# Fewer changes of TensorE tile shape per visit, and two constants moved, in an attention-then-MLP kernel

## The chip, the cores and the metric

The kernel runs on one core of a Trainium2 chip. The metric is the device time of one execution in microseconds (us). A profile of one more execution gives the span from the first to the last instruction, the busy time of each engine and every instruction's start. The engines are named PE (TensorE; PEld is its weight load), DVE (VectorE), ACT (ScalarE), POOL (GpSimd) and SP (SyncE, which here only issues transfers).

## What is computed

The reference is an attention of two parts for 64 heads (8 batches of 8 heads, 576 positions, 64 columns), summed, followed by an MLP with a SiLU gate on 4608 tokens of 512 columns.

```python
q_d, k_d, v_d = means of 4 neighbouring rows of q, k, v        # 144 positions
out_up    = repeat(softmax(q_d k_d^T / 8) v_d, 4)              # every 4 rows alike
mask      = abs(i - j) < 4                                     # a band, 576 x 576
out_local = softmax(where(mask, q k^T / 8, -1e9)) v
x   = (out_up + out_local) as (4608, 512)
h   = x @ w_in            # 512 -> 2048
out = (h * sigmoid(h)) @ w_out    # 2048 -> 512
```

## The kernel before

Heads go in pairs: 32 pairs p, each with its two heads h on the two halves of the 128 partitions. A pair passes through these steps. T(p) transposes q and k on TensorE into two banks of PSUM, which are evicted to qT and kT, and DVE or POOL sums groups of four columns into qd and kd. S(p) makes the band's scores and the coarse scores in the two banks of AB, and ACT takes the exponentials (Pt, Pd). Z(p) sums the exponentials with matmuls by 0/1 columns, and DVE takes the reciprocals of the sums (zr, 72 columns). PV(p) multiplies by v into the two banks of CD, and DVE multiplies CD by the reciprocals Rb, spread to all the rows that need them. POOL adds the two parts into xT, the MLP's input. VP(p) makes the coarse v of the first 14 pairs.

The whole plan is written as units with what they read and write; a list scheduler with estimated costs puts the units of each engine in an order before the program is made. A unit of an engine waits for what was written or read before it in the order in which the units were made. That holds for banks of PSUM too: the next writer of AB waits for the last reader of AB.

A matmul's tile shape (rows x columns of the array that it takes) follows from its operands. Half of the partitions on both sides gives 64x64, of which four run side by side. A whole contraction into half of the output gives 128x64. The MLP's matmuls are 128x128. S and PV before:

```python
def pe_S(u, p):
    ...
    for i in range(5):                       # the band: 20 matmuls of 64x64
        for h in range(2):
            for y in range(2):
                ...
                mm(u, AB[half(y), h, c:c + n], kT[j][half(h), t:t + 64], qT[j][half(h), t:t + n], rl, [rAB[h]])
    for h in range(2):                       # coarse, 4 of 64x64, 72 columns
        for y in range(2):
            mm(u, AB[half(y), h, 432:504], kd[j][half(h), 128:192], qd[j][half(h), 72 * y:72 * y + 72], rd, [rAB[h]])
    for h in range(2):                       # coarse, 2 of 64x128, 144 columns
        mm(u, AB[:, h, 288:432], kd[j][half(h), 0:128], qd[j][half(h), :], rd, [rAB[h]])

def pe_main(u, pv, z):
    ...
    if z is not None:                        # Z: 14 matmuls of 128x64 into CD[:, 0, 360:432]
        ...
    if pv is not None:                       # PV
        for y in range(2):                   # 4 of 128x64
            for h in range(2):
                mm(u, CD[half(h), y, 288:360], vd[n][:, 2 * h, :], Pd[m][:, h, 72 * y:72 * y + 72], rd, [rCD[y]], ...)
        for h in range(2):                   # 4 of 64x64
            for j in range(2):
                mm(u, CD[half(h), j, 288:360], vd[n][half(j), 2 * h + 1, :], Pd[m][half(j), h, 144:216], rd, [rCD[j]], ...)
        for i in range(5):                   # 20 of 64x64
            ...
```

How the reciprocals get spread depends on the pair. Pairs below NDIR = 8 split zr into three bf16 parts (one cast on ACT, three operations on DVE), and RB(p) spreads the parts by ten matmuls of 128x128 into AB, from where ACT copies them to Rb. For the others ACT's queue sends zr to memory and reads it back twice, once for each half of the partitions; the second transfer waits for the first, on ACT's own instruction stream.

```python
if p < NDIR:
    one("DVE", f"r{p}", ..., e.reciprocal(zs, CD[:, 0, 360:432]), ...)
    one("ACT", f"rh{p}", ...)       # h = bf16(zs)
    one("DVE", f"rx{p}", ...)       # the rest
    one("DVE", f"rm{p}", ...)       # m = bf16(rest)
    one("DVE", f"rl{p}", ...)       # l
    return
one("DVE", f"r{p}", ..., e.reciprocal(zr[i][:, :], CD[:, 0, 360:432]), ...)
dma("ACT", f"z{p}", scr[u][0:74, :], zr[i][0:74, :], ...)
for h in range(2):
    dma("ACT", f"b{p}", Rb[u][half(h), :], src, ..., r=[R(f"scr{u}")])
...
def RB(p):
    for m in range(10):
        mm(u, AB[:, x, 72 * c:72 * c + 72], sel[:, m, :], rpart[p % 2][:, 2, :], ..., [rAB[x]])
    one("ACT", f"eb{p}", 0.77, ... Rb[n] <- AB ..., r=rAB, w=[R(f"Rb{n}0"), R(f"Rb{n}1")])
```

The eviction of qT goes by ACT for pairs below NEQ = 8 and by DVE for the others: `eng = "ACT" if p < NEQ else "DVE"`. It reads the bank o0, which the second MLP matmul (G2) accumulates in as well.

Ten first rounds make the steps as single units (S(n), T(n+1), Z(n-1), PV(n-2), RB(n-1), VP(n-1) and, from n = 5, some of the first MLP matmuls G1). From n = 10 on, a visit n holds one unit V(n) and then MLP work:

```python
while todo or todo2:
    if n < NPAIR + 2:
        V(n)                 # S(n), T(n+1), Z(n-1), PV(n-2) in one unit
        if n <= NVP:
            VP(n - 1)
        feed()
    G1(1); G2((0,)); G1(1); G2((1,)); G1(1); G2((2, 3)); G1(1)
    n += 1
```

Of the kernel before, what the change touches and what calls it, by code (L numbers as in the profile page):

```python
# [16 lines left out]
NSUP = 9  # L17
XR = 1536
NVP = 14
NDIR = 8  # L20
NEQ = 8
NMQ = 8


# [251 lines left out]
def bass_hourglass_attn__then__act_silu_kernel(  # L276
# [9 lines left out]
    with kctx:  # L286
# [175 lines left out]
        def dma(eng, name, out_, in_, w, sem, dcost, r=(), prio=None, cost=0.42):  # L462
            return one(eng, name, cost, lambda s: s.dma_start(out_, in_), r, w, sem, prio, dcost)  # L463

        def load_qk(p):
            i = p % NQK
            ek = "ACT" if p < 1 else "SP"
            if p == 0:
                dma("ACT", "lkx", Rb[NR - 1][64:128, 0:576], bass.AP(tensor=k.tensor, offset=k.offset,
                                                                   ap=[[576, 64], [1, 576]]),  # L470
                    [R(f"Rb{NR - 1}1")], "kx", 0.5, prio=-20)
            dma("SP", f"lq{p}", qk[i][:, 0, :], bass.AP(tensor=q.tensor, offset=q.offset + 128 * p * 576,
                                                        ap=[[576, 128], [1, 576]]),
                [R(f"qk{i}0")], f"qk{i}0", 0.85, prio=10 * p)
            n = 128 if p < NPAIR - 1 else 64
            dma(ek, f"lk{p}", qk[i][0:n, 1, :], bass.AP(tensor=k.tensor, offset=k.offset + (128 * p + 64) * 576,
                                                          ap=[[576, n], [1, 576]]),
                [R(f"qk{i}1")], f"qk{i}1", 0.85, prio=10 * p)

        def load_v(p):  # L480
            i = p % NVS
            for h in range(2):
                n = 2 * p + h
                base = v[n // H_, n % H_]
                for j in range(2):
                    lo, hi = 0, 5
                    off = (288 * j - 3) * D_
                    w = [R(f"vs{i}{h}{j}")]
                    d = vs[i][half(j), 5 * h:5 * h + 5, :]
                    if n == 0 and j == 0:  # L490
                        lo = 1
                        one("DVE", "zero", 0.15, lambda g, d=d: g.memset(d[:, 0, :], 0.0), w=w)
                        first = bass.AP(tensor=base.tensor, offset=base.offset, ap=[[64, 61], [1, 64]])
                        dma("SP", f"lv{p}e", vs[i][3:64, 0, :], first, w, f"vs{i}{h}{j}", 0.3, prio=10 * p + 15)
                    if n == 2 * NPAIR - 1 and j == 1:
                        hi = 4
                        last = bass.AP(tensor=base.tensor, offset=base.offset + 517 * D_, ap=[[64, 59], [1, 64]])
                        dma("SP", f"lv{p}e", vs[i][64:123, 9, :], last, w, f"vs{i}{h}{j}", 0.3, prio=10 * p + 15)
                    win = bass.AP(tensor=base.tensor, offset=base.offset + off + 58 * 64 * lo,
                                  ap=[[64, 64], [58 * 64, hi - lo], [1, 64]])  # L500
                    dma("SP", f"lv{p}", d[:, lo:hi, :], win, w, f"vs{i}{h}{j}", 0.46, prio=10 * p + 15)

        def load_vq(p):
            b, h = divmod(2 * p, H_)
            i = p % NVQ
            base = v[b, h]
            t, o = base.tensor, base.offset
            dma("SP", f"lvq{p}", vq[i][:, 0:4:2, :],
                bass.AP(tensor=t, offset=o, ap=[[256, 128], [S_ * D_, 2], [1, 256]]),
                [R(f"vqm{i}")], f"vq{i}", 1.0, prio=10 * p + 21)  # L510
            for j in range(2):
                dma("SP", f"lvq{p}", vq[i][64 * j:64 * j + 16, 1:4:2, :],
                    bass.AP(tensor=t, offset=o + 128 * 256, ap=[[256, 16], [S_ * D_, 2], [1, 256]]),
                    [R(f"vqe{i}{j}")], f"vqe{i}{j}", 0.12, r=[R(f"vqc{i}1"), R(f"vqc{i}3")], prio=10 * p + 21)

        def load_w(c):
            if c < 4:
# [80 lines left out]
        def pe_S(u, p):  # L598
            j = p % NT
            rl = [R(f"kT{j}"), R(f"qT{j}"), R(f"kTp{j}0"), R(f"kTp{j}579")]  # L600
            rd = [R(f"kd{j}"), R(f"qd{j}"), R(f"kdp{j}")]
            for i in range(5):
                for h in range(2):
                    for y in range(2):
                        c, n = 58 * i, 58 if i < 4 else 56
                        t = 288 * y + c
                        mm(u, AB[half(y), h, c:c + n], kT[j][half(h), t:t + 64],
                           qT[j][half(h), t:t + n], rl, [rAB[h]])
            for h in range(2):
                for y in range(2):  # L610
                    mm(u, AB[half(y), h, 432:504], kd[j][half(h), 128:192], qd[j][half(h), 72 * y:72 * y + 72],
                       rd, [rAB[h]])
            for h in range(2):
                mm(u, AB[:, h, 288:432], kd[j][half(h), 0:128], qd[j][half(h), :], rd, [rAB[h]])

        def after_S(p):
            m = p % NP_
            one("ACT", f"x{p}", 0.66, lambda e: e.activation(Pt[m][:, :, :], AB[:, :, 0:288], AF.Exp, scale=0.125),  # L618
                r=rAB, w=[R(f"P{m}")])
            one("ACT", f"xd{p}", 0.54, lambda e: e.activation(  # L620
                Pd[m][:, :, :], AB[:, :, 288:504], AF.Exp, scale=0.0078125), r=rAB, w=[R(f"Pd{m}")])
            one("DVE", f"k{p}", 0.46, lambda e: e.tensor_tensor(
                Pt[m][:, :, :], Pt[m][:, :, :], mask_bf[:, :].unsqueeze(1).to_broadcast([128, 2, 288]), ALU.mult),
                r=[R(f"P{m}"), R("mask0"), R("mask1")], w=[R(f"P{m}")])
# [22 lines left out]
        def pe_main(u, pv, z):  # L647
            fresh = set()

            def first(x, h):  # L650
                f = (x, h) not in fresh
                fresh.add((x, h))
                return f

            if z is not None:
                m = z % NP_
                CD, rCD = acc(z)
                for s in range(4):
                    for h in range(2):
                        mm(u, CD[half(h), 0, 360:432], ohl[:, 63 - s:127 - s] if s else ohf[:, :],  # L660
                           Pt[m][:, h, 72 * s:72 * s + 72],
                           [R("ohl0"), R("ohl1"), R("ohf0"), R("ohf1"), R(f"P{m}")], [rCD[0]],
                           start=first(0, h), stop=False)
                for y in range(2):
                    for h in range(2):
                        mm(u, CD[half(h), 0, 360:432], ohp[:, 59 - 5 * y:123 - 5 * y], Pd[m][:, h, 72 * y:72 * y + 72],
                           [R("ohp"), R(f"Pd{m}")], [rCD[0]], start=False, stop=False)
                for h in range(2):
                    mm(u, CD[half(h), 0, 360:432], ohe[:, :], Pd[m][:, h, 144:216],
                       [R("ohe0"), R("ohe1"), R(f"Pd{m}")], [rCD[0]], start=False, stop=True)  # L670
            if pv is not None:
                m, n = pv % NP_, pv % NV
                CD, rCD = acc(pv)
                rd = [R(f"vd{n}0"), R(f"vd{n}1"), R(f"Pd{m}")]
                for y in range(2):
                    for h in range(2):
                        mm(u, CD[half(h), y, 288:360], vd[n][:, 2 * h, :], Pd[m][:, h, 72 * y:72 * y + 72],
                           rd, [rCD[y]], start=first(y, h), stop=False)
                for h in range(2):
                    for j in range(2):  # L680
                        mm(u, CD[half(h), j, 288:360], vd[n][half(j), 2 * h + 1, :], Pd[m][half(j), h, 144:216],
                           rd, [rCD[j]], start=False, stop=True)
                for i in range(5):
                    for h in range(2):
                        for j in range(2):
                            a, e = 58 * i, min(58 * i + 58, 288)
                            mm(u, CD[half(h), j, a:e], vb[n][half(j), 5 * h + i, :],
                               Pt[m][half(j), h, a:e], [R(f"vb{n}"), R(f"P{m}")], [rCD[j]],
                               start=False, stop=True)

        def after_Z(p):
            i, u = p % 2, p % NR
# [154 lines left out]
        def feed():  # L847

            for p in range(NPAIR):
                for name, fn, need in (  # L850
# [6 lines left out]
                        made.add((name, p))  # L857
                    if (name, p) in made or (src and (src, p) not in made):
                        continue
                    if p >= need[1] and (need[0], p - need[1]) not in made:  # L860
                        continue
                    if name in ("lv", "lvq") and ("lqk", p) not in made:
# [45 lines left out]
        while todo or todo2:  # L908
            if n < NPAIR + 2:
                V(n)  # L910
                if n <= NVP:
                    VP(n - 1)
                feed()
# [47 lines left out]
```

## Time and profile before

| | us |
|---|---|
| median of 3 runs | 368.88 (368.44 to 374.78) |
| span of the profiled execution | 369.2 |
| PE busy | 340.1 |
| DVE busy | 224.1 |
| ACT busy | 178.0 |
| POOL busy | 156.7 |

Times in the profile are from the first instruction. Busy time is a mean over stages that differ: the first rounds (up to about 76 us), the visits with attention and MLP (to about 290 us), and MLP alone. In a list of instructions in order of time each row has the start, the time to the end of the row's last instruction, the engine, the source line, the tiles (out<-in), the tile shape and operand, the number of instructions, and in brackets the idle time of the engine before it and what ended it. Matmuls are pipelined, so rows overlap; the distance between starts is what a step costs.

### The profile page before, as it was taken

To read this page: it belongs to the slowest core of one execution; us is meant where nothing else is said; L and a number is where in the kernel's file an instruction comes from. 1 tells how busy PE (TensorE), PEld (TensorE's weight loads), DVE (VectorE), ACT (ScalarE), POOL (GpSimd) and SP (SyncE) were. 2 spreads that over 40 slices of the span, in tenths; PEclk is the share of its full clock that TensorE was granted. 3 is DMA by queue.
4 is the path that set the end of the run, shared out by engine and by line. 5 is a ranking of instruction groups with operands and counts; after the bars stand their busy time and mean duration, and the time that the engine had idled before them with its cause. 6 is when DMAs were issued, how large, how long until landed. Compare 5 with 4: busy or idle time off the path is not lost.

```text
span 369.2 us, 10834 instructions
## 1 busy us (share of the span) xinstructions
PE 340.1 (92%) x4658; PEld 219.0 (59%) x4658; DVE 224.1 (61%) x390; ACT 178.0 (48%) x318; POOL 156.7 (42%) x203
## 2 busy tenths in 40 slices
PE   1684799889799999999999999999999999999996
PEld 0463577556466666666656666666656656666542
DVE  7574889877456677776777767777755343433400
ACT  3773677544255555445554554544443444443421
POOL 7838965543435555645565667453112100000000
PEclk9999589999899999999999999999999999999999
DMA  8898999999998767787768785322212110010012
GB/s 237 223 276 243 306 281 248 242 237 254 242 241 224 217 185 227 205 227 208 208 189 230 179 216 152 110 73 72 72 72 84 56 57 30 28 57 30 28 57 85
DMA packets 73977, 61.05 MB, mean 165 GB/s; under 512 B 48202, under 2 KB 56010, under 8 KB 73930
## 3 DMA queue, kind: packets, MB, share of 16 engines
q1 hardware_dynamic: 63818, 44.27, 44.9%
q10 hardware_dynamic: 5888, 9.80, 9.6%
q0 software_dynamic: 4224, 6.29, 7.5%
q8 instruction: 36, 0.59, 0.7%
q14 instruction: 11, 0.09, 0.1%
HBM read 52.49 MB, written 9.95 MB: 169 GB/s over the span
## 4 chain that ended last, share of the span: by engine, by line
PE 78%; DMA 8%; DVE 8%; POOL 2%; ACT 2%; ACTq 1%; issue 1%; POOLq 0%; DVEq 0%
PE HP L358 34%; PE o L358 25%; PE pe_ L358 8%; DMA scr<-zr 5%; PE CD L358 5%; PE AB L358 4%; DMA qk<-in_k_dram 3%; PE o L568 2%; POOL xo L381 2%; DVE rrest L702 1%; DVE gT L776 1%; DVE xo L736 1%; ACTq L463 1%; DVE rp L705 1%; DVE kd L582 1%
## 5 line engine op out<-in xcount | busy, mean ns | idle before, releaser
L358 PE MATMUL HP<-xT,w_in_sb 128*128 128x512 f32 x576 | 163.6, 421 | 1.1 <-DVE rp L705 1.0
L776 DVE SCALAR_TENSOR_TENSOR gT<-th,HP 128x512 bf16<-128x512 f32 x144 | 96.2, 683 | 102.3 <-ACT th L774 102.0
L774 ACT ACTIVATE th<-HP 128x512 f32<-128x512 f32 x144 | 85.9, 599 | 80.7 <-PE HP L358 78.8
L358 PEld LDWEIGHTS HP<-xT,w_in_sb 128*128 128x128 f32 x576 | 107.1, 192 | 27.6 <-DVE rp L705 1.1
L358 PE MATMUL o<-w_out_bf,gT 128*128 128x512 bf16 x464 | 107.2, 380 | 0.0
L358 PEld LDWEIGHTS o<-w_out_bf,gT 128*128 128x128 bf16 x464 | 42.4, 98 | 55.0 <-issue 9.5
L760 POOL TENSOR_TENSOR xT<-xo 128x576 fp32r<-128x576 f32 (+3 forms) x48 | 44.4, 938 | 51.3 <-DVE xo L736 51.1
L550 POOL CAST vb<-vs 128x640 bf16<-128x640 f32 x30 | 21.6, 719 | 68.1 <-PE CD L358 56.1
L791 ACT ACTIVATE osb<-o 128x512 f32<-128x512 f32 x29 | 17.3, 598 | 66.5 <-PE o L358 57.1
L540 POOL CAST qkb<-qk 128x1152 bf16<-128x1152 f32 x30 | 34.4, 1146 | 7.6 <-DMA qk<-in_k_dram 6.8
L568 PE MATMUL o<-idn,qkb 64*64 64x64 bf16 x576 | 17.4, 205 | 17.0 <-POOL qkb L540 7.5
L736 DVE TENSOR_TENSOR xo<-CD,Rb 128x720 f32<-128x720 f32 x30 | 27.1, 902 | 3.7 <-DMA Rb<-scr 2.3
L358 PE MATMUL pe_<-w_out_bf,gT 128*128 128x512 bf16 x112 | 26.4, 380 | 0.0
L568 PEld LDWEIGHTS o<-idn,qkb 64*64 64x64 bf16 x576 | 13.3, 117 | 20.6 <-POOL qkb L540 8.3
L578 ACT ACTIVATE kT<-pe_ 128x576 bf16<-128x576 bf16 x32 | 20.9, 654 | 8.6 <-PE pe_ L568 5.1
L555 POOL TENSOR_TENSOR vt<-vq 128x512 f32<-128x512 f32 x18 | 22.9, 1272 | 4.7 <-DMA vq<-in_v_dram 4.7
L582 DVE TENSOR_REDUCE kd<-kT 128x144 bf16<-128x576 bf16 x32 | 23.4, 734 | 1.5 <-ACT kT L578 1.5
L618 ACT ACTIVATE Pt<-AB 128x576 bf16<-128x576 f32 x32 | 20.8, 650 | 2.1 <-PE AB L358 1.9
L708 DVE RECIPROCAL zr<-CD 128x72 f32<-128x72 f32 x24 | 14.6, 607 | 8.4 <-PE CD L358 8.4
L568 PE MATMUL pe_<-idn,qkb 64*64 64x64 bf16 x576 | 16.7, 205 | 1.6 <-DVE qkb L537 1.0
L358 PEld LDWEIGHTS pe_<-w_out_bf,gT 128*128 128x128 bf16 x112 | 10.0, 98 | 13.6 <-issue 3.2
L586 DVE TENSOR_REDUCE qd<-qT 128x144 bf16<-128x576 bf16 x24 | 17.8, 743 | 0.0
(79 smaller groups left out, 313.8 us busy)
## 6 DMA issues: line engine op xcount, KB each, us to landing
vs<-in_v_dram SPq DMA_DIRECT2D x126, 80.0 KB, 4.2
qk<-in_q_dram SPq DMA_DIRECT2D x32, 288.0 KB, 4.6
out_dram<-osb SPq DMA_DIRECT2D x36, 256.0 KB, 2.9
qk<-in_k_dram SPq DMA_DIRECT2D x30, 288.0 KB, 5.2
Rb<-scr ACTq DMA_DIRECT2D x48, 180.0 KB, 4.4
vq<-in_v_dram SPq DMA_DIRECT2D x18, 256.0 KB, 5.3
w_in_sb<-in_moe_w_in_dram POOLq DMA_DIRECT2D x4, 1024.0 KB, 10.6
w_out_bf<-in_moe_w_out_dram POOLq DMA_DIRECT2D x4, 512.0 KB, 10.0
```

Source lines behind the costliest of these rows:

```text
L358: L.op(u, lambda t: t.matmul(out_, lhsT, rhs, start=start, stop=stop, skip_group_check=True), r, w)
L540: one("POOL", f"c{p}", 1.15, lambda g: g.tensor_copy(qkb[j][:, :, :], qk[i][:, :, :]), r=[R(f"qk{i}0"), R(f"qk{i}1")], w=[R(f"qkb{j}0"), R ...
L550: one("POOL", f"cw{p}", 0.72, lambda g: g.tensor_copy(vb[m][:, :, :], vs[i][:, :, :]), r=rr, w=[R(f"vb{m}")])
L555: one("POOL", f"va{p}", 1.3, lambda g: g.tensor_tensor(vt[:, :, :], vq[i][:, :, 0:128], vq[i][:, :, 128:256], ALU.add), r=rr, w=[R("vt")])
L568: L.op(u, lambda e, o=o, w=w, j=j: e.transpose(o, w, idn[half(j), :]), [R("id"), R(f"qkb{n}{x}")], [rE if x else rF])
L578: one("ACT", f"ek{p}", 0.68, lambda e: e.activation(kT[j][:, 3:579].rearrange("p (g r) -> p g r", r=9), pe_[:, 0:288].bitcast(BF16).rearra ...
L582: one("DVE", f"mk{p}", 0.74, lambda e: e.tensor_reduce(kd[j][:, 0:SD], kT[j][:, 3:579].rearrange("p (g r) -> p g r", r=4), AX.X, ALU.add), ...
L618: one("ACT", f"x{p}", 0.66, lambda e: e.activation(Pt[m][:, :, :], AB[:, :, 0:288], AF.Exp, scale=0.125), r=rAB, w=[R(f"P{m}")])
L736: one("DVE", f"m{p}", 0.92, prio=-450000 if L.boost else None, r=rCD + [R(f"Rb{u}0"), R(f"Rb{u}1")], w=[R(f"xo{x}")], fn=lambda e: e.tenso ...
L760: one("POOL", f"a{p}", 0.15 + n * 0.0019, lambda g, dst=dst, in0=in0, in1=in1: g.tensor_tensor(dst, in0, in1, ALU.add), r=[R(f"xo{x}")], w ...
L774: one("ACT", f"t{j}_{f}", 0.62, lambda e: e.activation(th[tb][:, :], hps[hb], AF.Tanh, scale=0.5), r=[rH[hb]], w=[R(f"th{tb}")], prio=-1)
L776: one("DVE", f"s{j}_{f}", 0.71, lambda e: e.scalar_tensor_tensor(gT[j % 2][:, f, :], th[tb][:, :], 1.0, hps[hb], ALU.add, ALU.mult), r=[rH ...
```

## The change

The change has three parts. It orders the matmuls of a visit by tile shape: in S the two matmuls of 64x128 become four of 64x64, and in the visit PV's 24 matmuls of 64x64 come ahead of Z, while PV's four of 128x64 come behind Z, whose shape they share. It raises NDIR from 8 to 10, so that pairs 8 and 9 are spread by TensorE as well (RB(9) is made right behind V(10)). It raises NEQ from 8 to 12, so that ACT evicts the q of pairs 8 to 11. A fourth piece would make the loads of late pairs wait (`tick`), from pair NTH on; with NTH = 99 and 32 pairs it never applies.

```diff
-NDIR = 8
-NEQ = 8
+NDIR = 10
+NEQ = 12
+NTH = 99
...
+        def tick(p, d):
+            return [R(f"tick{p - d}")] if p >= NTH else []
...                                     (tick(p, ...) added to the loads' reads)
             for h in range(2):
                 for y in range(2):
+                    mm(u, AB[half(y), h, 288:432], kd[j][half(h), 64 * y:64 * y + 64], qd[j][half(h), :], rd, [rAB[h]])
+            for h in range(2):
+                for y in range(2):
                     mm(u, AB[half(y), h, 432:504], kd[j][half(h), 128:192], qd[j][half(h), 72 * y:72 * y + 72],
                        rd, [rAB[h]])
-            for h in range(2):
-                mm(u, AB[:, h, 288:432], kd[j][half(h), 0:128], qd[j][half(h), :], rd, [rAB[h]])
...
+            if pv is not None:
+                ...
+                for h in range(2):
+                    for j in range(2):
+                        mm(u, CD[half(h), j, 288:360], vd[n][half(j), 2 * h + 1, :], Pd[m][half(j), h, 144:216],
+                           rd, [rCD[j]], start=first(j, h), stop=False)
+                for i in range(5):
+                    ...                         (the 20 band matmuls of PV, as before)
             if z is not None:
                 ...                             (Z, as before)
             if pv is not None:
                 ...
                 for y in range(2):
                     for h in range(2):
                         mm(u, CD[half(h), y, 288:360], vd[n][:, 2 * h, :], Pd[m][:, h, 72 * y:72 * y + 72],
-                           rd, [rCD[y]], start=first(y, h), stop=False)
-                ...                             (the 4 and the 20 matmuls of 64x64, moved up)
+                           [R(f"vd{n}0"), R(f"vd{n}1"), R(f"Pd{m}")], [rCD[y]], start=False, stop=True)
...
                 V(n)
+                if n <= NDIR:
+                    RB(n - 1)
                 if n <= NVP:
                     VP(n - 1)
```

More of the change, by code (lines that the diff above doesn't have):

```diff
@@ L473, in load_qk @@
                                                         ap=[[576, 128], [1, 576]]),
-                [R(f"qk{i}0")], f"qk{i}0", 0.85, prio=10 * p)
+                [R(f"qk{i}0")], f"qk{i}0", 0.85, r=tick(p, 4), prio=10 * p)
             n = 128 if p < NPAIR - 1 else 64
@@ L477, in load_qk @@
                                                           ap=[[576, n], [1, 576]]),
-                [R(f"qk{i}1")], f"qk{i}1", 0.85, prio=10 * p)
+                [R(f"qk{i}1")], f"qk{i}1", 0.85, r=tick(p, 4), prio=10 * p)
         def load_v(p):
@@ L500, in load_v @@
                                   ap=[[64, 64], [58 * 64, hi - lo], [1, 64]])
-                    dma("SP", f"lv{p}", d[:, lo:hi, :], win, w, f"vs{i}{h}{j}", 0.46, prio=10 * p + 15)
+                    dma("SP", f"lv{p}", d[:, lo:hi, :], win, w, f"vs{i}{h}{j}", 0.46, r=tick(p, 3), prio=10 * p + 15)
         def load_vq(p):
@@ L509, in load_vq @@
                 bass.AP(tensor=t, offset=o, ap=[[256, 128], [S_ * D_, 2], [1, 256]]),
-                [R(f"vqm{i}")], f"vq{i}", 1.0, prio=10 * p + 21)
+                [R(f"vqm{i}")], f"vq{i}", 1.0, r=tick(p, 3), prio=10 * p + 21)
             for j in range(2):
@@ L513, in load_vq @@
                     bass.AP(tensor=t, offset=o + 128 * 256, ap=[[256, 16], [S_ * D_, 2], [1, 256]]),
-                    [R(f"vqe{i}{j}")], f"vqe{i}{j}", 0.12, r=[R(f"vqc{i}1"), R(f"vqc{i}3")], prio=10 * p + 21)
+                    [R(f"vqe{i}{j}")], f"vqe{i}{j}", 0.12, r=[R(f"vqc{i}1"), R(f"vqc{i}3")] + tick(p, 3), prio=10 * p + 21)
         def load_w(c):
@@ L610, in pe_S @@
                 for y in range(2):
+                    mm(u, AB[half(y), h, 288:432], kd[j][half(h), 64 * y:64 * y + 64], qd[j][half(h), :], rd, [rAB[h]])
+            for h in range(2):
+                for y in range(2):
                     mm(u, AB[half(y), h, 432:504], kd[j][half(h), 128:192], qd[j][half(h), 72 * y:72 * y + 72],
                        rd, [rAB[h]])
-            for h in range(2):
-                mm(u, AB[:, h, 288:432], kd[j][half(h), 0:128], qd[j][half(h), :], rd, [rAB[h]])
         def after_S(p):
             m = p % NP_
+            made.add(("x", p))
             one("ACT", f"x{p}", 0.66, lambda e: e.activation(Pt[m][:, :, :], AB[:, :, 0:288], AF.Exp, scale=0.125),
-                r=rAB, w=[R(f"P{m}")])
+                r=rAB, w=[R(f"P{m}"), R(f"tick{p}")])
             one("ACT", f"xd{p}", 0.54, lambda e: e.activation(
@@ L653, in first @@
                 return f
+            if pv is not None:
+                m, n = pv % NP_, pv % NV
+                CD, rCD = acc(pv)
+                rd = [R(f"vd{n}0"), R(f"vd{n}1"), R(f"Pd{m}")]
+                for h in range(2):
[3 more added lines that the diff above has]
+                for i in range(5):
+                    for h in range(2):
+                        for j in range(2):
+                            a, e = 58 * i, min(58 * i + 58, 288)
+                            mm(u, CD[half(h), j, a:e], vb[n][half(j), 5 * h + i, :],
+                               Pt[m][half(j), h, a:e], [R(f"vb{n}"), R(f"P{m}")], [rCD[j]],
+                               start=False, stop=True)
             if z is not None:
@@ L673, in pe_main @@
                 CD, rCD = acc(pv)
-                rd = [R(f"vd{n}0"), R(f"vd{n}1"), R(f"Pd{m}")]
                 for y in range(2):
@@ L677, in pe_main @@
                         mm(u, CD[half(h), y, 288:360], vd[n][:, 2 * h, :], Pd[m][:, h, 72 * y:72 * y + 72],
-                           rd, [rCD[y]], start=first(y, h), stop=False)
[L679 to L689, printed above, removed]
+                           [R(f"vd{n}0"), R(f"vd{n}1"), R(f"Pd{m}")], [rCD[y]], start=False, stop=True)
         def after_Z(p):
@@ L859, in feed @@
                         continue
+                    if p >= NTH and name[0] == "l" and ("x", p - (4 if name == "lqk" else 3)) not in made:
+                        continue
                     if p >= need[1] and (need[0], p - need[1]) not in made:
```

## The prediction

> **What bounds the kernel now.** I read the slices of the page first, to see where TensorE is full.
>
> ```profile
> PE   1684799889799999999999999999999999999996
> DVE  7574889877456677776777767777755343433400
> PEclk9999589999899999999999999999999999999999
> ```
>
> Each digit is 9.2 us. From slice 11 (101 us) on PE has a 9 everywhere: the kernel ends when TensorE is through, and a nanosecond taken off PE there comes off the time. Before slice 8 it isn't full, and DVE shows 8 and 7. The granted clock falls twice, in slices 4 to 5 and in slice 10.
>
> Then the chain that ended last, for the stretch ahead of the full part and the first visits in it (start, length, what):
>
> ```profile
> 71.69 5.25 DMA scr<-zr
> 78.18 6.06 DMA scr<-zr
> 88.49 7.87 DMA scr<-zr
> 98.65 0.72 PE CD L358 x42
> 109.72 0.72 PE CD L358 x42
> 119.08 0.72 PE CD L358 x42
> ```
>
> Three transfers of reciprocals to memory stand in it, those of pairs 8, 9 and 10. From 98.65 on it is PE alone; the "CD x42" (Z and PV of one visit) come every 9 us or so, but the first distance is 11.07 us and the next 9.36.
>
> The instructions in order of time show what the third transfer does:
>
> ```profile
> 96.38 1.10 ACTq L463 DMA_DIRECT2D Rb<-scr  x2
> 97.52 0.60 ACT L791 ACTIVATE osb<-o 128x512 f32<-128x512 f32 x1 [6.69 <-issue]
> 98.17 0.21 PE L568 MATMUL o<-idn,qkb 64*64 64x64 bf16 x1 [2.48 <-ACT osb L791]
> ```
>
> ACT stands at the read-back, which waits for the landing, and is idle for 6.69 us. Behind it in ACT's order is the eviction that frees bank o0, in which visit 12's transposes want to write. PE idles 2.48 us. It is the only PE idle over 0.15 us after 76.29 us that I find until the end.
>
> Last, one visit on PE, with narrow windows so that the shapes come apart:
>
> ```profile
> 181.31 0.35 PE L358 MATMUL AB<-qT,kT 64*64 64x58 bf16 x20
> 181.49 0.21 PE L358 MATMUL AB<-qd,kd 64*64 64x72 bf16 x4
> ...
> 181.63 0.23 PE L358 MATMUL AB<-qd,kd 64*128 64x144 bf16 x2
> 181.79 0.21 PE L568 MATMUL o<-idn,qkb 64*64 64x64 bf16 x1
> ...
> 182.35 0.23 PE L358 MATMUL CD<-Pd,ohp 128*64 128x72 bf16 x4
> 182.41 0.20 PE L358 MATMUL CD<-Pd,ohe 128*64 128x72 bf16 x2
> 182.45 0.39 PE L358 MATMUL CD<-Pd,vd 128*64 128x72 bf16 x8
> ...
> 182.61 0.23 PE L358 MATMUL CD<-Pd,vd 64*64 64x72 bf16 x4
> 182.66 0.33 PE L358 MATMUL CD<-Pt,vb 64*64 64x58 bf16 x20
> 182.92 0.50 PE L358 MATMUL HP<-xT,w_in_sb 128*128 128x512 f32 x1
> ```
>
> Within one shape a step of 72 columns takes 0.03 us: four ohp, two at a time, from 182.35 to 182.41. Every change of shape has about 0.1 us more. From 181.49 to 181.63 there is one such step and 0.11 besides; 144 columns take twice 0.03, and from 181.63 to 181.79 there is 0.10 besides; two steps of vd should end at 182.51, and the 64x64 ones start at 182.61, 0.10 later. In addition the first four of the new shape hold up the next four: 182.61 to 182.66 is 0.05 instead of 0.03.
>
> [...] Here 2.48 us of idle were enough for the half clock of slice 10, and it costs the difference of the two distances above, 11.07 - 9.36 = 1.71 us. [...] the trace has 650 ns for the evictions of 576 columns on ACT, against 702 ns on DVE.
>
> **Part 1, the shapes.** A full visit before changes shape six times: 128x128 to 64x64 (S), 64x128, 64x64 (T), 128x64 (Z), 64x64 (PV), 128x128. After, three times: 64x64 (S, T, PV), 128x64 (Z, PV), 128x128. Gone are the three read above: 0.11 + 0.10 + 0.10 and twice 0.02 for the first four behind, less 0.01 for rounding: 0.34 us. The four 64x64 matmuls that take the place of two 64x128 run side by side in four quarters, so they take the same 0.06 us; I count nothing for them. Visits 11 to 30 are full: 20 x 0.34 = 6.8 us. Visit 31 has no T and goes from five changes to three: 0.24. Visits 32 and 33 have three either way. Visit 10 is in the full stretch of PE from its Z on (76.29 us): one change, 0.12. Sum 7.2 us, all on the path, as nothing in these visits lets PE idle.
>
> **Part 2, NDIR.** Pairs 8 and 9 no longer go through memory, but pair 10 still does. Its transfer took 7.87 us. Pair 9's read-backs, on the same queue, were issued at 84.26 and 84.75 and took 6.4 and 7.2 us, up to 92, so it stood behind them; pair 8's, with none in front of it, took 5.25. With some 5.25 the read-back would be issued near 93.8 and the eviction end near 95.5, just when PE arrives (95.7). I expect 85% of 2.48 + 1.71 = 4.2 us to go: 3.6 us.
>
> It costs: RB(9) is ten matmuls; the one of pair 7 took from 67.47 to 67.80, 0.33 us, at the same shape as its neighbours. I add 0.7 us in which PE waits for the third part of the reciprocals: the pairs before have such idle times of 0.21, 0.43, 0.53 and 0.96 us. Together 1.0.
>
> RB(8) is worse placed. It writes AB between S(9) and S(10), so visit 10 must wait for it and for ACT's copy out of AB (0.77 us). For pair 7 the reciprocal started at 61.45 and the third part was done at 66.25, 4.8 us. Pair 8's reciprocal starts at 71.05, so its third part comes at 75.85, RB at 76.2 and the copy with its hops at 77.2. S(10), which started at 73.86 before, starts at 77.3, and Z(9), which started at 76.29, comes 0.66 us behind it at 78.0: 1.7 us later. (From S to Z it is 182.20 - 181.31 = 0.89 us in the visit above, less the 0.23 us of S.) The MLP can't fill this: its first block is through by 74 us, its next one needs pair 7's x, and G2 needs a bank that visit 10's transposes use first.
>
> **Part 3, NEQ, and the first rounds.** From 58 to 77 us DVE is busy 16.6 of 19 us, ACT 10.7. Two evictions of 0.70 us leave DVE ahead of 71 us (in the rounds that make T(9) and T(10)), and one earlier (T(8)). Against it pair 8 brings DVE a mean of 0.86 + 0.27 + 0.65 = 1.8 us, but those are in the 4.8 us above already. S gets 0.24 us shorter in each round, where it is on the path only at times. I put 1.2 us for both: about half of the three evictions (1.0) and one S (0.2).
>
> Sum: -7.2 - 3.6 + 1.0 + 1.7 - 1.2 = -9.3. From 368.9 that makes **359.6 us**.
>
> **The rivals.** (a) The stop at visit 12 stays or moves to pair 10's new place, because the transfers are slow there for the other loads' sake (the DMA engines' share is 1.08 from 77 to 96 us). For it: 5.25 us is just the limit. Against it: pair 11's transfer, issued at 100.48, was followed by its read-back 3.9 us later. Then 3.6 us are lost: 363. (b) The wait for RB(8) brings a half clock of its own, 1.7 us or more, as 2.5 us of idle did twice: 361.5. Against it: RB and VP fall into that gap. (c) The handover at RB(8) is quicker, since ACT no longer stands still at 74.6 and DVE has two evictions less; then Parts 1 and 2 come whole: 356. (d) The shorter visits meet another bound, such as the reciprocals' way through memory, 11.5 us from zr at 174.08 to Rb at 185.6. Against it: CD must be free only 17 us after, and no engine but PE is over 72% busy from 103 to 223 us. Then perhaps 2 us of Part 1 are hidden: 361.6.
>
> **Range and chances.** Part 1 is read to some 0.02 us a visit, so it is good to 0.5 us. The rest has a spread of about 2.5 us, from (a) to (c). The range is 355.8 to 363.2. Two per cent are 7.4 us, a time of 361.5; Part 1 alone nearly gives that, and the rest is more likely a gain than a loss: 0.77 for faster, 0.22 for within 2%, 0.01 for slower.
>
> **What would show it.** In the profile after: full visits near 8.6 us apart in place of 8.96; no 64x128 group, and the 64x64 step ahead of the transposes without a 0.1 us hole; PE idle ahead of visit 10 with RB(8) or its copy as what ended it; no 2.48 us idle at visit 12 and no dip of the clock there; pair 10's transfer near 5 us. If the visits shrink by less than 0.3 us, Part 1 is wrong; if they do and the time is above 363, the stage from 70 to 100 us has a new stop.

## The result, and the profile after

| | us |
|---|---|
| before, median of 4 | 368.78 (368.44 to 374.78) |
| after, median of 4 | 360.38 (359.01 to 365.39) |
| ratio after to before | 0.976, 95% interval 0.973 to 0.979 |

The change makes the kernel 2.4% faster (2.1 to 2.7%). The medians are of all executions, while the ratios leave out those over 1.5% above the fastest of their kernel. The ratio times 368.8 is a gain of 8.7 us, between 7.7 and 9.9. The first profiled execution of the changed kernel was the longest of its timed ones (365.39 us), so the profile shown here is that of another execution of the same kernel (359.84 us, span 358.1).

The slices of the page, each 9.0 us wide now:

```profile
PE   1674899879999999999999999999999999999996
PEclk9995589999999999999999999999999999999999
```

The first digit is slice 0. PE is full from slice 9 on (81 us), before it was from slice 11, and the second dip of the clock is gone. The first is still there, in slices 3 and 4.

The chain that ended last (start, length, what), the Z and PV of visits 11 to 14:

```profile
86.15 0.61 PE CD L359 x39
95.19 0.61 PE CD L359 x39
104.30 0.61 PE CD L359 x40
113.34 0.61 PE CD L359 x40
```

The distances are 9.04, 9.11 and 9.04 us. Before, the distance from visit 12 to 13 was 11.07 and the next 9.36. No transfer of reciprocals stands in this stretch of the chain any more.

The instructions of one visit on PE, in order of time (visit 17; the transposes of T, from 139.20 on, are left out):

```profile
138.92 0.35 PE L359 MATMUL AB<-qT,kT 64*64 64x58 bf16 x20
139.10 0.27 PE L359 MATMUL AB<-qd,kd 64*64 64x144 bf16 x8
...
139.48 0.21 PE L359 MATMUL CD<-Pd,vd 64*64 64x72 bf16 x4
139.51 0.34 PE L359 MATMUL CD<-Pt,vb 64*64 64x58 bf16 x20
139.78 0.22 PE L359 MATMUL CD<-Pt,ohf 128*64 128x72 bf16 x2
...
140.00 0.20 PE L359 MATMUL CD<-Pd,ohe 128*64 128x72 bf16 x2
140.03 0.23 PE L359 MATMUL CD<-Pd,vd 128*64 128x72 bf16 x4
140.19 0.50 PE L359 MATMUL HP<-xT,w_in_sb 128*128 128x512 f32 x1
```

From the first score to the MLP it is 1.27 us; in the visit shown of before it was 182.92 - 181.31 = 1.61. The coarse scores, eight of 64x64 now, run straight into the transposes, the transposes into PV, and the last PV matmuls follow Z after 0.03 us. Only two steps inside the visit still have the 0.1 us: 64x64 to 128x64 (five bands of PV from 139.51 should end near 139.67, Z starts at 139.78) and 128x64 to 128x128.

### The profile page after: what moved, and what is told of

It is laid out like the page before. It is cut to its first block, busy times and chain, and to the rows that moved or that the text cites. A ratio compares the mean times of both kernels' runs of the same rounds, so it can differ in the third digit from the quotient of the medians.

```text
span 363.6 us, 10993 instructions
## 1 busy us (share of the span) xinstructions
PE 330.4 (91%) x4712; PEld 215.3 (59%) x4742; DVE 219.1 (60%) x392; ACT 182.2 (50%) x326; POOL 156.9 (43%) x203
## 4 chain that ended last, share of the span: by engine, by line
PE 88%; issue 4%; ACT 2%; SPq 2%; DVE 1%; DMA 1%; ACTq 0%
PE HP L359 40%; PE o L359 27%; PE pe_ L359 8%; PE CD L359 6%; PE AB L359 5%; SPq L464 2%; PE o L572 2%; DMA vs<-in_v_dram 1%; ACT Rb L735 1%; PE pe_ L572 1%; DVE rp L714 0%; ACT Pt L624 0%; DVE rp L713 0%; ACT Pd L626 0%; DVE xo L745 0%
## 5 line engine op out<-in xcount | busy, mean ns | idle before, releaser
L359 PE MATMUL o<-w_out_bf,gT 128*128 128x512 bf16 x437 | 101.7, 379 | 1.9 <-issue 0.2
L572 PEld LDWEIGHTS o<-idn,qkb 64*64 64x64 bf16 x576 | 14.1, 118 | 9.0 <-DVE qkb L539 6.3
L359 PEld LDWEIGHTS pe_<-w_out_bf,gT 128*128 128x128 bf16 x112 | 10.0, 98 | 13.6 <-issue 3.2
L626 ACT ACTIVATE Pd<-AB 128x432 bf16<-128x432 f32 x32 | 16.8, 526 | 0.0
## 6 DMA issues: line engine op xcount, KB each, us to landing
w_in_sb<-in_moe_w_in_dram POOLq DMA_DIRECT2D x4, 1024.0 KB, 10.2
```

Of the source, the lines that this page charges most:

```text
L359: L.op(u, lambda t: t.matmul(out_, lhsT, rhs, start=start, stop=stop, skip_group_check=True), r, w)
L572: L.op(u, lambda e, o=o, w=w, j=j: e.transpose(o, w, idn[half(j), :]), [R("id"), R(f"qkb{n}{x}")], [rE if x else rF])
```

## The experiments

The times of a group are medians from one chip, beside the kernel before on the same chip (of the kernel before again there is one execution). Gains are taken from the ratios.

| kernel | us | before beside it | ratio (95%) | visit 13 starts | 13 to 31 |
|---|---|---|---|---|---|
| changed, again | 360.32 | 369.11 | 0.979 (0.973 to 0.984) | 103.6 | 155.70 |
| shapes alone | 363.04 | 369.11 | 0.985 (0.978 to 0.993) | 104.4 | 155.66 |
| constants alone | 366.42 | 369.11 | 0.995 (0.992 to 0.997) | 105.0 | 161.55 |
| changed, NEQ = 8 | 361.30 | 369.11 | 0.981 (0.975 to 0.987) | 103.3 | 155.66 |
| before, again | 372.84 | 369.13 | | 110.7 | 161.39 |
| changed, two changes of shape put back | 365.12 | 369.13 | 0.988 (0.984 to 0.992) | 105.4 | 159.55 |
| changed, NDIR = 8 | 360.78 | 369.13 | 0.975 (0.970 to 0.981) | 103.0 | 156.33 |
| changed, NDIR = 12 | 360.26 | 369.13 | 0.976 (0.973 to 0.980) | 103.2 | 155.54 |
| before, S alone changed | 364.57 | 367.21 | 0.992 (0.989 to 0.995) | 101.8 | 157.66 |
| shapes alone, again | 361.91 | 367.21 | 0.981 (0.975 to 0.988) | 102.5 | 155.64 |
| changed, a third time | 358.51 | 367.21 | 0.976 (0.970 to 0.982) | 101.7 | 155.65 |
| changed, NMQ = 10 | 359.88 | 367.21 | 0.977 (0.971 to 0.982) | 104.2 | 155.72 |

"Visit 13 starts" and "13 to 31" are starts of S on PE in each kernel's one profile. In the first profile of before they are 108.8 and 161.39 us. What follows visit 31 takes 98.8 to 99.2 us in all of them. So a profile's time is the sum of these two columns and 99. The second of them is the same to 0.2 us within one order of shapes (one exception by 0.6), while the first scatters by some 2 us between executions of the same kernel.

**The changed kernel again**, without an edit.

> The changed kernel once more, unchanged, so that the parts can be set against it on the same chip. Both theories: 360.4 us as before, within 1 us. Its profile should have visits 8.64 us apart from visit 13 to 30 as in the first profile, and if the stop of 2.29 us at 88 us in that profile is no property of the kernel, it is missing or elsewhere here.

It measured 360.32 us, with visits 8.66 and 8.62 us apart (15 to 17). The stop at 88 us is missing, so it is no property of the kernel; what it coincides with stands in the last section.

**Only the order by shape.**

```diff
-NDIR = 10
-NEQ = 12
+NDIR = 8
+NEQ = 8
```

> Only the order by tile shape, with both constants at 8. Theory (the shapes carry nearly all of it, 0.31 us x 20 visits, and the constants give back in visit 10 what they save at visit 12): 362 us, with the 2.5 us stop and the half clock at visit 12 still there. Rival (the constants brought a third of the gain, as the prediction's sum has it, 2.1 of 9.3 us): 362.5 us or more. Second rival (the constants cost time): 359 us or less.

The median is 363.04 us, and the ratio gives a gain of 5.5 us (2.7 to 8.2). That can't tell the theory's 362 us from the first rival's 362.5 or more; the second rival is out. Its visits are those of the changed kernel. But the stop at visit 12 that the theory kept is not there, though pair 10 goes through memory right behind pair 9. ACT's instructions in this kernel:

```profile
88.23 0.23 ACTq L464 DMA_DIRECT2D scr<-zr  x1
92.90 1.10 ACTq L464 DMA_DIRECT2D Rb<-scr  x2
94.05 0.60 ACT L800 ACTIVATE osb<-o 128x512 f32<-128x512 f32 x1 [3.07 <-PE o L359]
```

The transfer lands after 4.7 us, and ACT then waits for PE's matmuls, not PE for ACT. The instructions of ACT, DVE, POOL and SP have the same order in this kernel as in the kernel before.

**Only the constants.**

```diff
-NDIR = 8
-NEQ = 8
+NDIR = 10
+NEQ = 12
...
                 V(n)
+                if n <= NDIR:
+                    RB(n - 1)
```

> Only the two constants (10 and 12, with the spreading of pair 9 behind visit 10), in the old order of shapes. Theory: 367 to 368 us, 1 to 2 us off the kernel before, with visits 8.96 us apart. Rival (constants bring a third): 366 us. Second rival (constants cost): 369 us or more.

It measured 366.42 us, a ratio of 0.995, so 2.0 us gained (1.0 to 2.9), and visits as long as before. The ratio puts that at the upper end of the theory's 1 to 2 us, the median of 366.42 us nearer to the first rival; the two aren't told apart. That the constants cost time is refuted.

**NEQ back at 8.**

```diff
-NEQ = 12
+NEQ = 8
```

> The changed kernel with q of pairs 8 to 11 evicted by VectorE again. Theory (VectorE is the tighter engine before 77 us, so its relief counts there): 1 to 1.5 us slower than the changed kernel, 361.5. Rival (the eviction's engine is off the path): the same, 360.4, within 0.5 us.

361.30 beside 360.32 us, with intervals that overlap by far: not settled by the time. The trace shows what the constant does around visits 9 and 10. In this kernel Z(8) comes behind S(9), as in the kernel before, and PE waits twice for the spreading of pair 8, first for VectorE's third part and then for ACT's copy out of AB:

```profile
71.79 0.50 PE L359 MATMUL AB<-rp,gT 128*128 128x72 bf16 x10 [0.80 <-DVE rp L714]
73.14 0.35 PE L359 MATMUL AB<-qT,kT 64*64 64x58 bf16 x20 [0.86 <-ACT Rb L735]
```

What that costs, and how the changed kernel escapes it, stands with RB(8) below.

**The kernel before again**, for a second profile.

> The kernel before once more, for a second profile. If the stop at visit 12 (2.48 us idle, then a half clock) belongs to the kernel, it is here again and visit 13 starts near 108.8 us. Rival (the landing of the transfer varies from run to run with what the queues hold, as the kernel with the shapes alone suggests, where pair 10 went through memory as well, its transfer took 4.7 us and PE did not stop): no stop, and visit 13 starts at 105 to 106 us; visits 8.96 us apart in either case.

The stop is there again. ACT and PE in this profile:

```profile
91.68 0.23 ACTq L463 DMA_DIRECT2D scr<-zr  x1
99.80 1.10 ACTq L463 DMA_DIRECT2D Rb<-scr  x2
100.95 0.60 ACT L791 ACTIVATE osb<-o 128x512 f32<-128x512 f32 x1 [6.62 <-issue]
101.60 0.21 PE L568 MATMUL o<-idn,qkb 64*64 64x64 bf16 x1 [2.41 <-ACT osb L791]
```

The transfer takes 8.1 us, as it took 7.9 in the first profile, and PE idles 2.41 us. No half clock follows here: the four MLP matmuls behind Z and PV take 1.20 us (from 102.81), where those under the half clock of the first profile took 2.08 (from 99.39). This profile has one more stop of that size: PE idles 2.24 us up to 88.17, since VectorE stands 4.29 us at pair 8's multiplication until its read-back from memory has landed, after 8.54 us; visit 13 starts at 110.7 us, later than in the first profile. The stop at visit 12 is there in both profiles of before, and in none of the eleven others shown in the table, four of which send pairs 8 to 10 through memory as well.

**Two changes of shape put back.** The blocks of the changed kernel in the order Z, PV's 64x64, PV's 128x64:

```diff
-            if pv is not None: ...   # PV, 24 of 64x64
             if z is not None: ...    # Z, 14 of 128x64
+            if pv is not None: ...   # PV, 24 of 64x64
             if pv is not None: ...   # PV, 4 of 128x64
```

> The changed kernel with two changes of shape put back: Z first, PV's 24 matmuls of 64x64 between Z and PV's four of 128x64. The same matmuls in number and size. Theory (each change costs 0.10 us plus 0.02, wherever it stands): full visits 0.24 us longer, 8.88 us, and the stretch from visit 13 to 31 4.3 us longer than the 155.7 us of the changed kernel; in all 5 us slower, 365.5. Rival (the gain came from the exchange of two matmuls of 64x128 for four of 64x64, or from where Z stands): visits stay near 8.64 us and the time near 360.4.

It measured 365.12 us, 1.2 points of ratio behind the changed kernel (0.976 in the result). The chain shows Z and PV of visits 14 and 15:

```profile
115.43 0.84 PE CD L359 x42
124.70 0.84 PE CD L359 x42
```

Each CD block takes 0.84 us where the changed kernel has 0.61, for the same 42 matmuls. From the first score to the MLP it is 1.51 us (the median of 17 visits), against 1.27: 0.117 us for each change of shape. Over 18 visits the stretch is 3.85 us longer, 0.21 a visit. The theory holds, with a size a little under its 0.24 us, and the rival's numbers are refuted: the four 64x64 matmuls are in this kernel too, and the time comes back all the same.

**NDIR back at 8**, NEQ at 12.

```diff
-NDIR = 10
+NDIR = 8
```

> The changed kernel with NDIR back at 8 (pairs 8 and 9 through memory), NEQ at 12. Theory (the spreading of two more pairs by TensorE is worth little by itself, as visit 10 then waits for it): within 1.5 us of the changed kernel, 361 to 362. Rival (the transfers of pairs 8 and 9 are what holds up the stage before visit 12): 363 or more.

360.78 us from four executions, no different from the changed kernel, as the theory has it: spreading two more pairs by TensorE is worth little in itself, once the evictions have moved.

**NDIR = 12.**

```diff
-NDIR = 10
+NDIR = 12
```

> The changed kernel with NDIR = 12: pairs 10 and 11 spread by TensorE as well, when the transfers are still dense. Theory (from visit 10 on PE is full and ACT no longer stands at a transfer, so each spread pair costs its 0.33 us and gains nothing): 361.0, 0.7 us slower than the changed kernel. Rival (the transfers before 100 us still cost PE waits and half clocks in many runs): 359.5 or less, and less spread between the runs.

360.26 us, the changed kernel's time. Neither the loss of 0.7 us nor a gain of one shows; the interval of the ratio is 1.4 us wide to each side, so a loss of 0.7 isn't excluded.

**S alone**, in the kernel before.

```diff
+            for h in range(2):
+                for y in range(2):
+                    mm(u, AB[half(y), h, 288:432], kd[j][half(h), 64 * y:64 * y + 64], qd[j][half(h), :], rd, [rAB[h]])
             for h in range(2):
                 for y in range(2):
                     mm(u, AB[half(y), h, 432:504], ...)
-            for h in range(2):
-                mm(u, AB[:, h, 288:432], kd[j][half(h), 0:128], qd[j][half(h), :], rd, [rAB[h]])
```

> The kernel before with the change in S alone: four matmuls of 64x64 for the two of 64x128, all else as before, constants at 8. Theory (two changes of shape fewer, each 0.10 us, and one slow first step): full visits 8.96 - 0.23 = 8.73 us, the stretch from visit 13 to 31 161.4 - 18 x 0.23 = 157.3 us, in all 4.6 us faster than the kernel before, 364.5. Rival (only the removal of all three changes together lets TensorE run on): less than half of that, 367 or more.

One visit on PE in this kernel (transposes left out):

```profile
137.81 0.35 PE L358 MATMUL AB<-qT,kT 64*64 64x58 bf16 x20
137.99 0.27 PE L358 MATMUL AB<-qd,kd 64*64 64x144 bf16 x8
...
138.78 0.39 PE L358 MATMUL CD<-Pd,vd 128*64 128x72 bf16 x8
139.00 0.33 PE L358 MATMUL CD<-Pt,vb 64*64 64x58 bf16 x20
139.26 2.10 PE L358 MATMUL HP<-xT,w_in_sb 128*128 128x512 f32 x8
```

The CD part still has its hole; the AB part has none. This block takes 1.45 us, one of two longer ones; the median is 1.387 us, 0.226 less than the 1.613 of before, and the stretch from 13 to 31 is 157.66, 0.21 a visit less. So two thirds of a visit's gain are S's, one third PV's. The time is 364.57 us, a gain of 2.9 us (1.9 to 4.0): less than the 4.6 expected. Half of 4.6 lies inside that interval, so it is the trace, with 0.23 us off each block, that refutes the rival, and not the time.

**The shapes alone again**, beside the changed kernel.

> The order by shape alone once more (constants at 8), beside the changed kernel on the same chip: what do the constants bring on top of the shapes? Theory (the shapes alone already take the stop at visit 12 away, so the constants add only some 1 to 2 us ahead of visit 11): 361.5 to 363, the changed kernel 360.4. Rival (they add as much as they do without the shapes, and the stop besides): 364 or more.

> The changed kernel for the third time, to set the two beside it against: 360.4, within 1 us.

361.91 and 358.51 us; the changed kernel came out 1.9 us below what was expected, as did the kernel before beside it (367.21). By the ratios the constants bring 1.9 us here on top of the shapes, and 2.5 us beside the first run of the shapes alone, with intervals that overlap both times. That is nearer to the theory's 1 to 2 us than to the rival, whose 364 us aren't reached. The stop at visit 12 is absent from this profile of the shapes alone as well (pair 10's transfer: 4.9 us).

**NMQ = 10.**

```diff
-NMQ = 8
+NMQ = 10
```

> The changed kernel with NMQ = 10 in place of 8: qd of pairs 8 and 9 is summed by GpSimd (two operations, 1.2 us) instead of VectorE (0.74 us). Theory (VectorE still sets the pace from 45 to 73 us, so taking 1.5 us off it shows): 359.5, 0.8 us faster than the changed kernel. Rival (with the evictions gone VectorE no longer is the bound, or GpSimd's casts come later and hold the transposes up): 360.4 or slower.

359.88 beside 358.51 us: no gain. This profile has a wait of 2.21 us at 76.07, in which PE waits for GpSimd's sum into xT; taking work off VectorE gave it to the engine that the MLP waits for. None of the versions beats the changed kernel.

## Why the prediction was right, term by term

**Part 1, right: 7.2 us predicted, about 6.7 found.** The block of a visit went from 1.613 to 1.274 us, 0.339, as predicted. Over visits 13 to 30 the gain is 161.39 - 155.70 = 5.69 us, 0.316 a visit. In three of these visits the block takes 1.38 to 1.40 us, because TensorE stops inside the 64x64 bands of PV, which the kernel before never does there; that takes 0.35 us off. Visits 11 and 12, at 0.34 each, add 0.68, and from visit 31 on 0.25 is gained (99.06 to 98.81; predicted 0.24). I count the prediction's 0.12 for visit 10 unmeasured: 5.69 + 0.68 + 0.25 + 0.12 = 6.7. Both halves of it were shown by themselves, S in one experiment and the order of Z and PV in another.

**Part 2, the stop: it went, but not for the reason given.** From visit 12 to 13 the profiles of before take 13.6 and 12.0 us, all others 9.1 to 9.4; less the 0.34 of Part 1 that is 4.2 us in the first, which has the half clock there, and 2.6 in the second, where 3.6 were predicted. But the step "with none in front of it ... 5.25" made the stop a matter of pair 9's read-backs on the queue. With those read-backs still in front, pair 10's transfer took 4.7, 4.9, 4.9 and 5.2 us in the four kernels with NDIR = 8 and some or all of the new shapes, and PE didn't stop. Without them it took 2.3 to 4.5. So they do cost time, but not the stop. What adds 3 us to the transfer in the old order of shapes, with the same order of instructions on the other four engines, stays open. And both profiled executions of before (371.0 and 372.8 us) are slower than most timed ones, so the stop is perhaps not in all of them: the prediction took it for a fixed part of the 368.9 us. The timed runs agree: by the ratios the shapes alone gain 5.5 and 7.0 us, about what Part 1 gives, although their profiles lack the stop. The 3.6 us for it don't show there.

**Part 2, RB(8): the wait came, the loss didn't.** The prediction had visit 10 wait for ACT's copy out of AB. It does, in all profiles with NDIR of 10 or more. On PE, around visits 9 and 10 of the changed kernel:

```profile
67.40 0.22 PE L359 MATMUL CD<-Pt,ohf 128*64 128x72 bf16 x2
68.25 0.35 PE L359 MATMUL AB<-qT,kT 64*64 64x58 bf16 x20
72.26 0.50 PE L359 MATMUL AB<-rp,gT 128*128 128x72 bf16 x10
73.77 0.35 PE L359 MATMUL AB<-qT,kT 64*64 64x58 bf16 x20 [1.01 <-ACT Rb L735]
```

PE idles 1.01 us ahead of S(10), and it is ACT's copy that ends it. But the step "Pair 8's reciprocal starts at 71.05" failed. In the changed kernel Z(8) is placed ahead of S(9) (67.40 and 68.25; before, Z at 70.58 came behind S at 68.98). The reciprocal starts at 67.86, and its third part is done 3.5 us later, not 4.8. Besides, the old wait of 1.47 us in visit 10 for VectorE's multiplication is gone.

It is NEQ that moves Z(8): it comes ahead of S(9) in every profile with NEQ = 12 and behind it in every one with NEQ = 8. So the stretch to compare is the one from RB(7) to the MLP behind visit 10's CD block. It takes 9.5 and 9.4 us in the two profiles of before, and 9.4 in both of the shapes alone. With NDIR = 10 and NEQ = 8 it takes 10.9: there the loss comes, 1.5 us, of which I put 0.8 down to a half clock right behind the two waits (from S(10) to the MLP 2.23 us; 1.40 and 1.28 in the changed kernel), as rival (b) of the prediction had it. The changed kernel takes 9.2 and 10.2 us, with VP(8)'s 0.5 us inside, which the others make ahead of RB(7): 0.7 us gained and 0.3 lost, where 1.7 were to be lost. The prediction counted NEQ's evictions and NDIR's waits as separate terms, and didn't see that the one changes the order on which the other rests.

**Part 2, RB(9): 1.0 predicted, about 0.3 measured.** It takes its 0.33 us, and PE shows no wait for the third part. The idle time of 0.96 us that I had put down to such a wait (66.42 us in the first profile of before) stands ahead of matmuls of the MLP, which don't read the third part (last section).

**Part 3: 1.2 predicted, not seen.** S(9) starts at 69.0 and 68.6 us before, at 68.3 and 66.9 after, and anywhere from 66.0 to 70.8 in the other experiments, without regard to the constants. What NEQ did was to move Z(8).

So the 9.3 us of the sum came near the 8.7 measured partly by luck. Part 1 came as read and carries most of it. The losses of 2.7 us in Part 2 came to little (0.7 won or 0.3 lost at RB(8), 0.3 lost at RB(9)), and the 3.6 + 1.2 us of gain in Parts 2 and 3 came to less than that as well. The constants bring 2.0 us by themselves and 1.9 to 2.5 on top of the shapes, where Parts 2 and 3 gave them 2.1. Which of the two constants brings it isn't settled: NEQ = 12 alone on top of the shapes has a ratio of 0.975, NDIR = 10 alone 0.981, with intervals that overlap. Of what they bring on top of the shapes, 0.8 us is seen in the profiles: visit 13 starts at 103.6 and 101.7 us against 104.4 and 102.5. The rest isn't located. A part may be the clock: the old wait in visit 10, 1.3 to 1.6 us long, has a half clock behind it in two of the five profiles that show the wait: the second of before (mean granted clock 0.966, against 0.981 in the first) and the first of the shapes alone, where the eight MLP matmuls from 76.02 take 3.25 us, against 2.07 from 87.58. The 1.01 us in its place has none in the three of the changed kernel (2.11 us for the eight matmuls from 75.17 in the second of them).

## What to carry to other kernels

On a full TensorE, look for steps between starts that are longer than the stream of the matmul: each change of tile shape stood there as 0.10 us and a slow first step, and it was saved by ordering the matmuls, and by cutting a larger tile into smaller ones that run side by side (the coarse scores and the step behind them took 0.30 us with two of 64x128, 0.10 with 64x64 alone). Read such gains from a stretch that repeats; here 0.34 us a visit were read and 0.34 measured. A stop that stands once in one profile, by contrast, ought to be looked for in a second profile before it goes into a sum, and a wait that a change adds may only take the place of one that was there. Where a scheduler sets the order, the parts of a change don't simply add: here one constant moved the matmuls from which the cost of the other was worked out.

## What the runs showed of the hardware

In a visit of before (181.31 us), four matmuls of 64x64 start within 0.01 us of one another, and the next four, of 58 columns, 0.03 us behind them; of 128x64 and of 64x128 two start together like that.

Changes of shape cost about the same in every direction seen, in the first profiles of before and of the changed kernel. At 64x64 to 64x128, 64x128 to 64x64, 64x64 to 128x64, 128x64 to 64x64, and from 64x64 and 128x64 to 128x128, the first matmul of the new shape starts 0.12 to 0.16 us after the last of the old one, where the next group of the same shape starts 0.02 to 0.06 us after it: about 0.10 us more each time (64x128 has only one group, so the step of 64x64 with the same 144 columns stands for it). From 128x128 to 64x64 it is 0.32 us in place of 0.23.

TensorE also stops in the midst of a group, with no wait in the trace, for instance inside PV's bands in the kernel with NDIR = 12:

```profile
28.88 0.34 PE L359 MATMUL CD<-Pt,vb 64*64 64x58 bf16 x6
31.39 0.31 PE L359 MATMUL CD<-Pt,vb 64*64 64x58 bf16 x14 [2.17 <-issue]
```

Six of the twenty matmuls start, and the others 2.17 us later. The trace's DMA records have packets of 16 KB of the kind "instruction" on queue 8, 36 in the kernel before and 37 after, one about every 8 us. In the eleven profiles of the experiments other than that of the kernel before there are 23 such stops of more than 0.15 us that nothing but "issue" ends; 22 of them end 1.27 to 1.71 us after the end of such a packet, against 6 of the 178 stops there that something else is seen to end. In the changed kernel's first profile there are six, and they end 1.23 to 1.54 us after a packet; the one of 2.29 us at 88 us is among them (1.41), and four of the six lie before 61 us. The 0.96 us idle at 66.42 us in the first profile of before ends 1.52 us after a packet. What TensorE waits for in these stops was not shown: no experiment took the packets away, so this is a coincidence in time and not more. Since the stops move from execution to execution (the one at 88 us is missing in the changed kernel's second profile), they may be one source of the spread of the times.
